# Eight cos/sin tables issued by ScalarE, the x pieces alone in SyncE's queue, and new instruction orders, in a spectral mixer with a gated FFN on one core

## The chip, the core and the metric

The kernel runs on one core of one Trainium2 chip. The metric is the device time of one execution in microseconds, as the median of several runs. A further execution is recorded by the hardware profiler; its own time stands beside its span below, since all durations come from it.

## The reference

The input x has 2048 rows of 576 numbers (bf16). Two blocks follow one another, each on a layer norm and with a residual:

```python
def _A_ref(x, w_r, w_i):
    X = rfft2(x.astype(float32), axes=(-2, -1))
    X = X * (w_r + 1j * w_i)
    return irfft2(X, s=(S, D), axes=(-2, -1)).astype(bfloat16)

def _B_ref(x, w_gate, w_up, w_down):
    return (gelu(x @ w_gate) * (x @ w_up)) @ w_down      # 576 -> 4608 -> 576

h  = x + _A_ref(layernorm(x), w_r, w_i)
h2 = h + _B_ref(layernorm(h), w_gate, w_up, w_down)
```

## The kernel before

The rows lie as 128 partitions by 16 tiles (tile c holds row 16p + c on partition p), in the buffer `XO`. Both Fourier transforms and their inverses are matrix products with tables of cosines and sines. The work has these stages, one behind the other with overlap:

- **First transform, groups 0 to 5** (`GROUPS`: tiles 0-1, 2-3, 4-6, 7-9, 10-12, 13-15). The layer norm is folded into the table: per tile, the mean and variance are found, the group's reciprocal of the standard deviation is taken, and the table `ATB` is multiplied by it into `ATS`. PE then multiplies x with `ATS` (line 537). Negated and tail copies of x go to `XN` for that.
- **Spectral stage**, 16 groups of frequencies: D (line 611) multiplies with `FT`, B (621) with `BT`, T, Z on VectorE apply the weights `WS` (w, line 635, makes their negated copy, in four parts `w0` to `w3`), V (651) and R (663) go back with `VT`.
- **Inverse and second norm** for the first six tiles: the matmuls of line 736 and 779, then transposes.
- **FFN** in four blocks of 512 rows: gate and up products (line 877), Gelu on ScalarE, product on VectorE, down product (line 978). The other ten tiles' inverse is done inside the first block.

Nothing is scheduled at run time. Each engine executes its instructions in the order in which the program records them, and a recording layer (`Prog`) turns reads and writes of named keys into semaphore waits. Three strings give the order. `LORD` lists the first loads: `x0-2` is the piece of x with tiles 0 and 1, `a0-4` the tables of tiles 0 to 3. `SEQ1` orders the first transform, `SEQF` the spectral stage. A word of `SEQ1` is a letter, a number and sometimes an engine (A ScalarE, D VectorE, P GpSimd):

| word | what it records | line |
|---|---|---|
| B, b | statistics of the first and second half of a tile, VectorE | 480 |
| S, Q | sum and sum of squares of a tile on ScalarE (tiles 3, 4, 13) | 472, 476 |
| m | the squared mean of such a tile | 483 |
| v, q, c | aggregate (VectorE), square root (ScalarE), reciprocal (VectorE) of a group | 489/492, 496, 501 |
| n, t | negated copy and tail copy of a group's x, GpSimd | 553, 558 |
| x | scaling of a group's tables, GpSimd (P) or VectorE (D) | 506, 511 |
| M | matmuls of a group | 537 |
| E, F | eviction of a finished bank (F: its second half, late) | 548 |
| k | idle matmuls on zeros: `k14` is 14 of them | 522 |

All loads before the FFN weights are issued by SyncE in one queue: the words of `LORD`, then `FT` and `BT`, the spectral weights in two halves, `VT`, `DT`, `IT`, `DP`, `ITD`, `IDT`. ScalarE issues no DMA. Its first instruction is a one-element square root (line 431), ahead of which the activation table is loaded. Two small constants, `EXQ` and `MK` (six memsets, lines 417 to 420), are set by VectorE; `EPT` and `ZD` by GpSimd.

Of the kernel before, what the change touches and what calls it, by code (L numbers as in the profile page):

```python
# [9 lines left out]
S, D, K2 = 2048, 576, 289  # L10
# [10 lines left out]
NPRE = 6  # L21
PARTS = ((0, 256), (256, 512))
GROUPS = ((0, 2), (2, 4), (4, 7), (7, 10), (10, 13), (13, 16))
SEQ1 = """S3 B0 t1 b0 b1 B1 v0 q0 c0 Q3 n0 m3D B2 k14 t0 x0P b2 n1 v1 q1 n2 k104 c1 B5 S4 m4P b5 Q4 B6 M0 E1A b6 v2 B7 x1P E0A M1 E4A q2 E5A t2 b7 c2 B9 E3A x2P E2A E8A E6A b8 S13 B8 b9 v3 q3 k202 M2 B11 B10 n3 n4 c3 x3P E12A b10 b12 E9A b11 B12 v4 E13A Q13 E7A q4 E10A t3 E11A B15 m13P E14A M3 t4 c4 E15A E16A b14 x4P M4 B14 b15 t5 v5 E17D q5 E18A E21A n5 E19A c5 x5D E20D E22D E23A E24A F23A F24A M5 E27A E25D E29A F29A E26D E28D F28A F25D F27D F22A F26D""".split()
LORD = "x0-2 x2-4 a0-4 x4-8 a4-8 x8-12 x12-16 a8-16".split()
SPLIT = tuple(int(w[1:-1]) for w in SEQ1 if w[0] == "F")
ACT_TILES = tuple(int(w[1:]) for w in SEQ1 if w[0] == "Q")
SEQF = """D0 D1 w0 D2 B0 T0 D3 B1 Z0 D4 T1 Z1 B2 V0 T2 B3 D5 T3 B4 D6 w1 Z2 T4 Z3 D7 B5 D8 w3 B6 w2 D9 T5 Z4 B7 Z5 T6 B8 R0 D11 T7 V2 Z7 D10 V1 B9 T8 B10 D13 Z6 V4 T9 T10 R1 D12 V3 Z8 B11 B12 Z9 D14 T11 V6 B13 T12 V5 B14 Z11 V7 Z10 T13 D15 Z12 T14 V8 Z13 V9 B15 Z14 R2 T15a V12 V10 T15b Z15a V11 Z15b V13 V14 R3 V15 R4""".split()
VENG = [('act',), ('act',), ('act',), ('act',), ('act',), ('act',), ('act',), ('act',), ('act',), ('act',), ('act',), ('act',), ('act',), ('act',), ('act',), ('act', 'act')]
DENG, BENG = ['act', 'act', 'act', 'act', 'act', 'act', 'act', 'act', 'act', 'act', 'act', 'act', 'act', 'act', 'act', 'act'], ['act', 'act', 'act', 'act', 'act', 'act', 'act', 'act', 'act', 'act', 'act', 'act', 'act', 'act', 'act', 'act']  # L30
SEQ = """I0 I1 N0 I2 s0 N1 I3 S1 q0 N2 I4 c0 e0 s2 q1 n0 n1 N3 I5 c1 z0 n2 s3 e1 D1 N4 N5 e2 q2 c2 n3 e3 D2 g10 g00 h10 z3 h00 g20 g01 h20 h01 g21 g11 h21 h11""".split()
# [281 lines left out]
def _build(nc, A_x, A_w_r, A_w_i, B_w_gate, B_w_up, B_w_down, out):  # L313
    P = Prog(nc)
    T = build_tables()
    dram = {n: nc.inline_tensor(_np_bf16(T[n]), name="c_" + n.lower()) for n in T}
    PE, DVE, ACT, SP, POOL = "pe", "dve", "act", "sp", "pool"
# [4 lines left out]
    XO = sb.alloc("XO", [128, NT, D], BF16)  # L322
# [35 lines left out]
    EXQ = sb.alloc("EXQ", [128, NT], F32)  # L358
    NM = sb.alloc("NM", [128, NT], F32)
    MK = sb.alloc("MK", [128, 4], F32)  # L360
# [24 lines left out]
    ATB = sb.alloc("ATB", [128, NT, 128], BF16)  # L385
# [28 lines left out]

    P.op(POOL, lambda g: g.memset(EPT[:, :], EPS), w=["EPT"])
    P.op(POOL, lambda g: g.memset(ZD[:, :], 0.0), w=["ZD"])
    P.op(DVE, lambda g: g.memset(EXQ[:, :], -0.5), w=["EXQ"])
    P.op(DVE, lambda g: g.memset(MK[:, :], 0.0), w=["MK"])
    for j in range(4):
        P.op(DVE, lambda g, j=j: g.memset(MK[32 * j:32 * j + 32, j:j + 1], 1.0), w=["MK"])  # L420
    xv = A_x[0].rearrange("(p c) d -> p c d", c=NT)
    ov = out[0].rearrange("(p c) d -> p c d", c=NT)
    tabs = dram["ATAB"].rearrange("p (c k) -> p c k", c=NT)

    def x_load(i, c0, c1, eng):
        P.dma(eng, XO[:, c0:c1, 0:D], xv[:, c0:c1, :], f"ld{i}", w=[("X", c) for c in range(c0, c1)])

    def atb_load(i, c0, c1, eng):
        P.dma(eng, ATB[:, c0:c1, :], tabs[:, c0:c1, :], f"ld{i}", w=[("ATB", c) for c in range(c0, c1)])

    P.op(ACT, lambda a: a.activation(SA[:, 0, 0:1], EPT[:, 0:1], ACTF.Sqrt), r=["EPT"], w=[("SA0", 0)])
    for i, w in enumerate(LORD):
        c0, c1 = (int(v) for v in w[1:].rstrip("@").split("-"))
        (x_load if w[0] == "x" else atb_load)(i, c0, c1, ACT if w[-1] == "@" else SP)
    P.dma(SP, FT[:, :, :].rearrange("p a b -> p (a b)"), dram["FTAB"][:, :], "ft", w=["FT"])
    P.dma(SP, BT[:, :, :, :].rearrange("p a b c -> p (a b c)"), dram["BTAB"][:, :], "bt", w=["BT"])

# [41 lines left out]
    def ln1_half(c, h):  # L479
        P.op(DVE, lambda v: v.bn_stats(ST1[:, c, h, :], XO[:, c, 288 * h:288 * h + 288]), r=[("X", c)], w=[("ST1", c, h)])  # L480
# [59 lines left out]
    def a_ev(n, eng, late=False):  # L540
        i, k = n // 5, AORD[n % 5]
        hs = (1,) if late else (0,) if n in SPLIT else (0, 1)
        g0, g1 = 8 * hs[0], 8 * hs[-1] + 8
        c0, c1 = GROUPS[i]
        m, b = c1 - c0, a_bank(i, k)
        src = bank(b, 0, 128, 0, 128 * m).rearrange("p (n g e) -> p n g e", n=m, g=16)[:, :, g0:g1, :]
        dst = U[:, k, g0:g1, c0:c1, :].rearrange("p g n e -> p n g e")
        fn = (lambda v: v.tensor_copy(dst, src)) if eng == DVE else (lambda a: a.activation(dst, src, ACTF.Copy))  # L548
        P.op(eng, fn, r=[("PS", b)] + ([("EV", n)] if late else []), w=[("U", i, k, h) for h in hs] + ([] if late else [("EV", n)]))
# [12 lines left out]
    RUN1 = {"k": idle_mm, "S": act_sum, "Q": act_sq, "B": lambda c: ln1_half(c, 0), "b": lambda c: ln1_half(c, 1), "v": ln1_var, "q": ln1_sqrt, "c": ln1_rs, "M": a_mm, "x": ln1_scale, "E": a_ev, "F": lambda n, eng: a_ev(n, eng, True), "n": x_neg, "m": act_mean2, "t": x_tail}  # L562
    for w in SEQ1:
        a = w[1:]
# [3 lines left out]
    c = 0  # L568
    while c < NT:
        c1 = c + 1  # L570
        while c not in ACT_TILES and c1 < NT and c1 not in ACT_TILES:
            c1 += 1
        src, f, keys = (SA[:, 0, c:c1], -1.0 / D, "SA0") if c in ACT_TILES else (MV1[:, c:c1, 0], -1.0, "MV1")
        P.op(POOL, lambda g, c=c, c1=c1, src=src, f=f: g.tensor_scalar(NM[:, c:c1], src, f, 1.0, op0=ALU.mult, op1=ALU.mult),
             r=[(keys, k) for k in range(c, c1)], w=[("NM", k) for k in range(c, c1)])
        c = c1
# [5 lines left out]
    FB, used = {}, [0] * 8  # L582
    for t, w in enumerate(SEQF):
        k, i = w[0], w[1:].rstrip("abc")
        if k in "DB":
            late = ("V", 0) in FB or any(x[0] == "V" for x in SEQF[t:t + 4])
            b = min((0, 2, 4) if late else (0, 2, 4, 6), key=lambda b: max(used[b], used[b + 1]))
            used[b] = used[b + 1] = t + 1
        elif k in "VR":
            b = min((6, 7) if ("D", LAST) not in FB else range(8), key=lambda b: used[b])  # L590
            used[b] = t + 1
            if k == "V":
                b2 = b
                if int(i) == LAST and len(VENG[LAST]) > 1:
                    b2 = min(range(8), key=lambda b: used[b])
# [79 lines left out]

    for w in SEQF:
        i = int(w[1:].rstrip("abc"))
# [43 lines left out]
    for t, w in enumerate(SEQ):  # L721
        k, i = w[0], int(w[1:])
# [294 lines left out]
def bass_sequential_preLN__spectral_gfnet__geglu_ffn__prompt_kernel(  # L1017
    nc, A_x, A_w_r, A_w_i, B_x, B_w_gate, B_w_up, B_w_down, out
):
    _build(nc, A_x, A_w_r, A_w_i, B_w_gate, B_w_up, B_w_down, out)  # L1020
# [28 lines left out]
```

## Time and profile before

| what | value |
|---|---|
| median of 3 runs | 490.87 us (490.7 to 491.16) |
| the profiled execution | 491.02 us |
| its span, first to last instruction | 489.2 us |
| PE busy | 481.8 us, 98% |
| VectorE, ScalarE, GpSimd busy | 193.6, 150.7, 32.1 us |
| granted PE clock, mean | 1.000 |
| read from HBM, written | 26.22 MB, 2.36 MB |

A line of a timeline gives the start in microseconds from the span's start, the duration, the engine, the line of the program, the operation, what is written and read, and in brackets how long the engine stood idle before it and what ended that. The durations shown overlap a little on ScalarE and VectorE: an eviction of 0.65 us (line 603) is followed by the next at 0.55 us. The chain of waits is followed back from the last instruction, at each step to what released it.

### The profile page before, as it was taken

The page shows a single profiled execution, that of the slowest core. Times are in us where ns is not written, and L with a number is a line of the kernel's source. Part 1 is how long each engine was busy: PE and PEld are TensorE (multiplying, and loading weights), DVE is VectorE, ACT ScalarE, POOL GpSimd, SP SyncE. Part 2 cuts the span into 40 slices and gives each one's busy share as a digit, 9 for nine tenths or more (in the row PEclk, how much of TensorE's full clock was granted, in tenths as well). Part 3 has the DMA queues.
Part 4 walks back from the last instruction along what each step waited for, and adds up shares of the span by engine and source line. Part 5 has one row for each costly group of instructions (what it writes and reads, how often), then busy time and mean ns, then how long its engine had stood idle before and what let it go on. Part 6 is the DMA issues. An engine that isn't in the chain of part 4 may idle for free.

```text
span 489.2 us, 9939 instructions
## 1 busy us (share of the span) xinstructions
PE 481.8 (98%) x4376; PEld 286.3 (59%) x4376; DVE 193.6 (40%) x399; ACT 150.7 (31%) x297; POOL 32.1 (7%) x60
## 2 busy tenths in 40 slices
PE   7899999999999999999999999999999999999998
PEld 3787754444688744444577644444677544444775
DVE  6799733433576634433311144333211233333111
ACT  6999742233322223323200032233100122323000
POOL 5511441000000020000000000000000000000000
PEclk9999999999999999999999999999999999999999
DMA  8990999100001071100000001000000000000000
GB/s 283 231 325 16 365 366 340 26 15 2 1 19 40 13 233 23 24 4 1 2 18 19 13 20 22 16 0 1 7 19 19 7 1 0 1 2 1 13 20 18
DMA packets 25148, 31.20 MB, mean 64 GB/s; under 512 B 11440, under 2 KB 17840, under 8 KB 25104
## 3 DMA queue, kind: packets, MB, share of 16 engines
q1 hardware_dynamic: 22208, 18.62, 13.4%
q0 software_dynamic: 2896, 11.95, 7.0%
q8 instruction: 34, 0.56, 0.5%
q14 instruction: 10, 0.08, 0.1%
HBM read 26.22 MB, written 2.36 MB: 58 GB/s over the span
## 4 chain that ended last, share of the span: by engine, by line
PE 92%; ACT 3%; DVE 3%; DMA 1%; issue 0%; SPq 0%; POOL 0%; DVEq 0%
PE PS L877 57%; PE PS L978 29%; PE PS L537 1%; DMA XO<-in_A_x_dram 1%; DVE TP L630 1%; PE PS L895 1%; ACT V L603 1%; PE PS L736 1%; ACT YS L603 1%; PE PS L611 1%; PE PS L779 1%; PE PS L913 1%; ACT U L548 0%; DVE VR L666 0%; ACT CUS L603 0%
## 5 line engine op out<-in xcount | busy, mean ns | idle before, releaser
L877 PE MATMUL PS<-HT,WG 64*128 64x512 bf16 (+1 forms) x2160 | 228.7, 371 | 0.0
L877 PEld LDWEIGHTS PS<-HT,WG 64*128 64x128 bf16 x2160 | 105.0, 94 | 121.9 <-issue 0.7
L886 DVE TENSOR_TENSOR AT<-GL,PS 128x512 bf16<-128x512 bf16 (+1 forms) x147 | 99.4, 677 | 177.9 <-ACT GL L885 177.9
L885 ACT ACTIVATE GL<-PS 128x512 bf16<-128x512 f32 (+1 forms) x147 | 86.5, 588 | 262.6 <-PE PS L877 251.3
L978 PE MATMUL PS<-WD,AT 128*128 128x288 bf16 (+2 forms) x1152 | 144.9, 286 | 0.0
L978 PEld LDWEIGHTS PS<-WD,AT 128*128 128x128 bf16 x1152 | 110.7, 98 | 30.6 <-ACT GL L885 0.8
L877 PE MATMUL PS<-HT,WGX 64*128 64x512 bf16 x486 | 53.4, 376 | 0.0
L981 DVE TENSOR_TENSOR OS<-PS,XO 128x288 bf16<-128x288 f32 (+2 forms) x32 | 14.6, 457 | 94.4 <-PE PS L978 94.3
L877 PEld LDWEIGHTS PS<-HT,WGX 64*128 64x128 bf16 x486 | 23.7, 94 | 28.8
L611 PE MATMUL PS<-FT,U 128*128 128x288 bf16 x96 | 13.9, 286 | 0.0
L630 DVE TENSOR_TENSOR TP<-YS,WS 128x1152 bf16<-128x1152 bf16 (+2 forms) x17 | 12.0, 719 | 2.7 <-ACT YS L603 2.5
L900 ACT ACTIVATE EB<-PS 128x288 f32<-128x288 f32 x10 | 4.1, 411 | 27.6 <-PE PS L895 27.6
L537 PE MATMUL PS<-ATS,XO 128*128 128x128 bf16 x96 | 8.6, 219 | 3.1 <-POOL ATS L506 1.6
L480 DVE BATCH_NORM_STATS2 ST<-XO 128x6 f32<-128x288 bf16 x26 | 10.0, 441 | 2.7 <-DMA XO<-in_A_x_dram 2.7
L918 DVE TENSOR_TENSOR XO<-PS,XO 128x576 bf16<-128x576 f32 x10 | 7.6, 756 | 8.0 <-PE PS L913 8.0
L611 PEld LDWEIGHTS PS<-FT,U 128*128 128x128 bf16 x96 | 9.2, 98 | 2.3
L603 ACT ACTIVATE CUS<-PS 128x576 bf16<-128x576 f32 x16 | 10.4, 659 | 0.5 <-PE PS L611 0.3
L603 ACT ACTIVATE YS<-PS 128x576 bf16<-128x576 f32 x16 | 10.3, 664 | 0.4 <-DVE TP L630 0.4
L621 PE MATMUL PS<-CUS,BT 128*128 128x288 bf16 x64 | 10.0, 286 | 0.0
L548 ACT ACTIVATE U<-PS 128x256 bf16<-128x256 f32 (+2 forms) x29 | 9.6, 417 | 0.7 <-PE PS L537 0.6
L906 DVE TENSOR_TENSOR QB<-PS,EB 128x288 f32<-128x288 f32 x20 | 8.2, 452 | 3.3 <-ACT EB L900 3.3
L823 DVE TENSOR_SCALAR HN<-XO,NM,RS 128x576 bf16<-128x576 bf16 (+1 forms) x28 | 9.2, 369 | 0.1
(80 smaller groups left out, 207.6 us busy)
## 6 DMA issues: line engine op xcount, KB each, us to landing
WD<-in_B_w_down_dram POOLq DMA_DIRECT2D x9, 576.0 KB, 12.0
WG<-in_B_w_up_dram SPq DMA_DIRECT2D x4, 1152.0 KB, 7.8
WG<-in_B_w_gate_dram POOLq DMA_DIRECT2D x4, 1152.0 KB, 10.2
out_dram<-OS SPq DMA_DIRECT2D x30, 72.0 KB, 1.6
XO<-in_A_x_dram SPq DMA_DIRECT2D x3, 576.0 KB, 7.4
WGX<-in_B_w_up_dram SPq DMA_DIRECT2D x1, 1152.0 KB, 6.0
WGX<-in_B_w_gate_dram POOLq DMA_DIRECT2D x1, 1152.0 KB, 10.0
HT<-HN SPq DMA_TRANSPOSE x60, 2.4
```

The lines of the kernel that those rows point to most:

```text
L480: P.op(DVE, lambda v: v.bn_stats(ST1[:, c, h, :], XO[:, c, 288 * h:288 * h + 288]), r=[("X", c)], w=[("ST1", c, h)])
L537: P.op(PE, lambda t, b=b, lhs=lhs, s=s, e=e, o=o, c=c: t.matmul(bank(b, 0, 128, o, o + 128), lhs, ATS[:, c, :], start=s, stop=e), r=[("X", ...
L548: fn = (lambda v: v.tensor_copy(dst, src)) if eng == DVE else (lambda a: a.activation(dst, src, ACTF.Copy))
L603: fn = (lambda v: v.tensor_copy(dst, src)) if eng == DVE else (lambda a: a.activation(dst, src, ACTF.Copy))
L611: P.op(PE, lambda t, b=b, m=m, us=us, o=o: t.matmul(bank(b, 0, 128, 0, 2 * HK), U[:, us, i, :, :], FT[:, 3 * o + (2 if us == 4 else us // ...
L621: P.op(PE, lambda t, b=b, tb=tb, m=m, s3=s3, sp_=sp_: t.matmul(bank(b, 0, 128, 0, KW), BT[:, sp_, tb, :], CUS[:, s3, m, :], start=(m == 0) ...
L630: P.op(DVE, lambda v: v.tensor_tensor(TP[:, tl, :, :, q0:q1], y4, w4, op=ALU.mult), r=[("Y", sl), ("Wn", i)] + (wkeys[0] if 1 <= g < 9 els ...
L877: op = P.op(PE, lambda t, h0=h0, kt=kt, wt=wt, b=b, s=(not second and j == 0), e=(second and j == n - 1): t.matmul(bank(b, 0, 128, c0, c1) ...
L885: P.op(ACT, lambda a: a.activation(GL[:, s2, c0:c1], bank(b0, 0, 128, c0, c1), ACTF.Gelu_apprx_tanh), r=[("PS", b0)], w=[("GL", s2)])
L886: P.op(DVE, lambda v: v.tensor_tensor(AT[:, f, c0:c1], GL[:, s2, c0:c1], bank(b0 + 1, 0, 128, c0, c1), op=ALU.mult), r=[("GL", s2), ("PS", ...
L978: P.op(PE, lambda t, b=b, d0=d0, d1=d1, f=f, p=p: t.matmul(bank(b, 0, 128, 0, d1 - d0), AT[:, f, 128 * p:128 * p + 128], WD[:, f, d0:d1], ...
L981: P.op(DVE, lambda v, b=b, d0=d0, d1=d1, p=p, c=c: v.tensor_tensor(OS[:, p % 2, d0:d1], bank(b, 0, 128, 0, d1 - d0), XO[:, c, d0:d1], op=A ...
```

## The change

1. `LORD` is new. SyncE's queue now has x0-2, x2-4, x4-8, x8-12, the tables 8-16, x12-16. The tables 0-4 and 4-8 are issued by ScalarE; a new read key makes them wait for the one-element square root.
2. The six memsets of `EXQ` and `MK` go from VectorE to GpSimd.
3. `SEQ1` and `SEQF` have new orders. The number of instructions of each kind stays the same; the squared mean of tile 3 goes from VectorE to GpSimd (`m3D` to `m3P`), and the evictions are dealt out anew between ScalarE and VectorE.

```diff
-SEQ1 = """S3 B0 t1 b0 b1 B1 v0 q0 c0 Q3 n0 m3D B2 k14 t0 x0P b2 n1 v1 q1 n2 k104 c1 B5 S4 m4P b5 Q4 B6 M0 E1A b6 v2 B7 x1P E0A M1 E4A q2 E5A t2 b7 c2 B9 E3A x2P E2A E8A E6A b8 S13 B8 b9 v3 q3 k202 M2 B11 B10 n3 n4 c3 x3P E12A b10 b12 E9A b11 B12 v4 E13A Q13 E7A q4 E10A t3 E11A B15 m13P E14A M3 t4 c4 E15A E16A b14 x4P M4 B14 b15 t5 v5 E17D q5 E18A E21A n5 E19A c5 x5D E20D E22D E23A E24A F23A F24A M5 E27A E25D E29A F29A E26D E28D F28A F25D F27D F22A F26D""".split()
-LORD = "x0-2 x2-4 a0-4 x4-8 a4-8 x8-12 x12-16 a8-16".split()
+SEQ1 = """S3 n0 b0 B0 b1 t1 B1 v0 q0 b2 c0 Q3 n1 B2 m3P v1 q1 B6 k104 t0 x0P t2 c1 x1P b5 B7 k14 S4 B5 m4P Q4 b6 B8 M0 E4A E1A E0A v2 M1 E7A E3A B9 q2 b7 E9A c2 E2A n2 E8A E6A b8 S13 B11 b9 v3 q3 b10 k202 E5A n3 B12 x2P c3 M2 E10A E11A t4 Q13 t3 B10 b11 b12 v4 q4 m13P E13A x3P b15 c4 b14 E14A B14 B15 n4 x4P v5 E12A M3 E16A E15A E17D q5 E18A c5 n5 x5D M4 E20D E19A E22A E23A F23A E21D t5 M5 E25A E27D E24A F24D E29D E26A F25A F26D F27D E28A F29D F22D F28A""".split()
+LORD = "x0-2 x2-4 x4-8 x8-12 a8-16 x12-16 a0-4@ a4-8@".split()
...
-SEQF = """D0 D1 w0 D2 B0 T0 D3 B1 Z0 D4 T1 Z1 B2 V0 T2 B3 D5 T3 B4 D6 w1 Z2 T4 Z3 D7 B5 D8 w3 B6 w2 D9 T5 Z4 B7 Z5 T6 B8 R0 D11 T7 V2 Z7 D10 V1 B9 T8 B10 D13 Z6 V4 T9 T10 R1 D12 V3 Z8 B11 B12 Z9 D14 T11 V6 B13 T12 V5 B14 Z11 V7 Z10 T13 D15 Z12 T14 V8 Z13 V9 B15 Z14 R2 T15a V12 V10 T15b Z15a V11 Z15b V13 V14 R3 V15 R4""".split()
+SEQF = """D1 w1 w0 D0 D2 B1 B0 T1 T0 Z0 D3 D4 Z1 B2 D5 w3 T2 w2 B3 T3 Z3 B4 T4 D6 B5 D8 D7 B6 V0 Z4 V1 Z2 T5 B7 T6 B8 Z6 R0 D9 V2 D10 V3 T7 B9 Z5 T8 Z7 B10 D11 T9 V4 Z9 T10 D12 R1 B11 Z8 T11 V6 D13 Z11 B12 T12 D14 B13 V5 Z10 T13 B14 V7 T14 Z12 D15 V8 Z13 V9 Z14 B15 R2 V10 T15a V13 V11 T15b Z15a Z15b V14 V12 R3 V15 R4""".split()
...
-    P.op(DVE, lambda g: g.memset(EXQ[:, :], -0.5), w=["EXQ"])
-    P.op(DVE, lambda g: g.memset(MK[:, :], 0.0), w=["MK"])
+    P.op(POOL, lambda g: g.memset(EXQ[:, :], -0.5), w=["EXQ"])
+    P.op(POOL, lambda g: g.memset(MK[:, :], 0.0), w=["MK"])
     for j in range(4):
-        P.op(DVE, lambda g, j=j: g.memset(MK[32 * j:32 * j + 32, j:j + 1], 1.0), w=["MK"])
+        P.op(POOL, lambda g, j=j: g.memset(MK[32 * j:32 * j + 32, j:j + 1], 1.0), w=["MK"])
...
-        c0, c1 = (int(v) for v in w[1:].rstrip("@").split("-"))
-        (x_load if w[0] == "x" else atb_load)(i, c0, c1, ACT if w[-1] == "@" else SP)
+        c0, c1 = (int(v) for v in w[1:].rstrip("@!").split("-"))
+        (x_load if w[0] == "x" else atb_load)(i, c0, c1, ACT if w[-1] in "@!" else SP, {"@": [("SA0", 0)], "!": [("X", 0)]}.get(w[-1], []))
```

More of the change, by code (lines that the diff above doesn't have):

```diff
@@ L423, in _build, with x_load, atb_load @@
     tabs = dram["ATAB"].rearrange("p (c k) -> p c k", c=NT)
[L425 to L429, printed above, removed]
+    def x_load(i, c0, c1, eng, r):
+        P.dma(eng, XO[:, c0:c1, 0:D], xv[:, c0:c1, :], f"ld{i}", r=r, w=[("X", c) for c in range(c0, c1)])
+    def atb_load(i, c0, c1, eng, r):
+        P.dma(eng, ATB[:, c0:c1, :], tabs[:, c0:c1, :], f"ld{i}", r=r, w=[("ATB", c) for c in range(c0, c1)])
     P.op(ACT, lambda a: a.activation(SA[:, 0, 0:1], EPT[:, 0:1], ACTF.Sqrt), r=["EPT"], w=[("SA0", 0)])
     for i, w in enumerate(LORD):
-        c0, c1 = (int(v) for v in w[1:].rstrip("@").split("-"))
-        (x_load if w[0] == "x" else atb_load)(i, c0, c1, ACT if w[-1] == "@" else SP)
+        c0, c1 = (int(v) for v in w[1:].rstrip("@!").split("-"))
+        (x_load if w[0] == "x" else atb_load)(i, c0, c1, ACT if w[-1] in "@!" else SP, {"@": [("SA0", 0)], "!": [("X", 0)]}.get(w[-1], []))
     P.dma(SP, FT[:, :, :].rearrange("p a b -> p (a b)"), dram["FTAB"][:, :], "ft", w=["FT"])
```

## The prediction

> **What bounds the kernel now.** I read the page first, then the chain of waits in order of time, then POOL's timeline, then the DMA rate by stretches.
>
> ```profile
> span 489.2 us, 9939 instructions
> PE 92%; ACT 3%; DVE 3%; DMA 1%; issue 0%; SPq 0%; POOL 0%; DVEq 0%
> ```
>
> PE carries the chain, and a change that removes no matmul can gain only where the chain leaves PE. The chain in order of time shows where that is.
>
> ```profile
> 2.11 5.87 DMA XO<-in_A_x_dram
> 7.98 0.02 issue
> 8.01 1.55 DVE ST L480 x4
> 9.56 0.62 POOL ATS L506
> ...
> 15.27 4.83 PE PS L537 x81
> 20.10 2.21 PE PS L611 x18
> ...
> 48.34 1.63 PE PS L736 x12
> ```
>
> Columns: start, length, what. The first link is the third x piece (tiles 4 to 7), issued at 2.11 and landed at 7.98. From 48.34 on PE runs almost without a break to the end at 489.2, in an order that the change leaves alone. So the change is worth what it does to the start of the first L736 matmul, 48.34. That stretch has two parts: up to the first L611 matmul (19.93 in the timeline), and 28.4 us after it.
>
> The chain view hides who paces the first part. POOL's timeline shows it (start, length, line, tile, idle before):
>
> ```profile
> 8.06 0.91 POOL L553 TENSOR_SCALAR XN<-XO 128x864 bf16<-128x864 bf16 x1 [0.54 <-DMA XO<-in_A_x_dram]
> 9.14 0.26 POOL L483 TENSOR_SCALAR TM<-SA 128x1 f32<-128x1 f32 x1 [0.18 <-POOL XN L553]
> 9.56 0.61 POOL L506 TENSOR_TENSOR ATS<-ATB,RS 128x256 bf16<-128x256 bf16 x1
> 10.26 0.27 POOL L558 TENSOR_SCALAR XN<-XO 128x96 bf16<-128x96 bf16 x1
> 10.82 0.83 POOL L506 TENSOR_TENSOR ATS<-ATB,RS 128x384 bf16<-128x384 bf16 x1 [0.29 <-DVE RS L501]
> 11.81 0.91 POOL L553 TENSOR_SCALAR XN<-XO 128x864 bf16<-128x864 bf16 x1 [0.16 <-POOL ATS L506]
> ...
> 13.96 0.83 POOL L506 TENSOR_TENSOR ATS<-ATB,RS 128x384 bf16<-128x384 bf16 x1 [0.17 <-POOL XN L553]
> 14.88 0.27 POOL L558 TENSOR_SCALAR XN<-XO 128x96 bf16<-128x96 bf16 x1
> ...
> 16.02 0.83 POOL L506 TENSOR_TENSOR ATS<-ATB,RS 128x384 bf16<-128x384 bf16 x1
> ```
>
> From the landing at 7.98 to the scaling of group 4 (x4P, 16.02) POOL only pauses 0.08 (one wait) or about 0.16 (several) between instructions, and once 0.29. PE starts that group at 16.91 and goes on to 19.93: 3.91 us behind x4P's start. Hence x4P's start sets the first part, and the landing of x tiles 4 to 7 sets x4P.
>
> Why that piece lands at 7.98 shows in the DMA rates (last number, GB/s; the one before, DMA share):
>
> ```profile
> 2.50:4.25 1.75, 1.75 (x5) 0.61 (x4) 0.56 (x2) 0.00 (x0) 0.00 (x0) 1.00 1.21 380
> 4.25:5.25 1.00, 1.00 (x3) 0.30 (x2) 1.00 (x4) 0.78 (x2) 0.57 (x2) 1.00 0.56 104
> 5.25:8.00 2.75, 2.75 (x20) 1.50 (x19) 1.68 (x9) 1.25 (x4) 1.88 (x4) 1.00 0.95 339
> 8.00:12.50 4.50, 2.65 (x40) 2.08 (x38) 4.49 (x18) 4.28 (x14) 3.58 (x6) 1.00 1.02 400
> ```
>
> There is a hole from 4.25 to 5.25. Issue start plus time to landing, asked issue by issue, gives: x0-2 3.67, x2-4 4.44, tables 0-4 4.74, x4-8 7.98, tables 4-8 8.76, x8-12 10.46, x12-16 11.91, tables 8-16 12.57. The hole begins where the queue goes from the first tables to x4-8.
>
> **The change part by part.**
>
> *SyncE's queue.* Two issues of 0.47 us go from ahead of x8-12, one of them from ahead of x4-8, so x4-8 is issued 0.47 and x8-12 0.95 earlier. That alone brings nothing: the engines were moving earlier pieces. What counts is the bytes ahead and the hole. Ahead of x4-8, after x2-4, there stood 131 kB of tables; now up to 262 kB come through the other queue beside it. Early end: no hole, 262 + 590 kB at 400 GB/s from 4.44 = 6.6. Late end: the hole stays and 131 kB more pass, 7.98 + 0.33 = 8.3. The nearest row is x12-16, an x piece directly behind an x piece as x4-8 now is: 1.45 us. With 0.3 for each table (as tables 0-4 took) that is 4.44 + 2.05 = 6.5. I take at most 7.0. FT, BT and the weights move about 0.9 us up; they landed from 14.6 to 26.5, before their first use, and are worth nothing. Without that cover the next is the negation w3, which moves from 29.65 to about 25 and needs the weights that landed at 24.40: 0.6 us of cover.
>
> *ScalarE's queue.* Two issues behind the 0.20 us Sqrt that ends at 2.22. No row shows a DMA issued by ACT; SP's rows are 0.43, POOL's up to 0.98. ACT then is free at 3.1 to 4.2, and its next instruction waits for x at 4.46: nothing, with 0.3 us of cover at the worst end. Tables 0-4 are issued 0.6 later than before (2.25 for 1.64). POOL needs them at 6.4, before they landed 3.1 after issue: 5.4. One microsecond of cover.
>
> *Memsets.* Six tiny ones move from DVE to POOL, 0.06 to 0.1 each and 0.08 apart, ending near 2.5. POOL first works on x at 3.75. Nothing; 1.2 us of cover.
>
> *POOL's order.* It now runs n0, t1, n1, m3P, t0, x0P, t2, x1P, m4P, n2, n3, x2P, t4, t3, m13P, x3P, n4, x4P. m3P is new on POOL (0.26 and a pause of 0.16); t4 comes ahead of x4P as before. x1P has two predecessors:
> - On POOL: n0 ends at 4.42, t1 starts at 4.6 (x2-4 at 4.44; 4.8 if the tables push it to 4.74). t1 0.24, n1 0.67, m3P 0.26, t0 0.24, x0P 0.61, t2 0.27 are 2.29; six pauses of 0.08 or 0.16 are 0.8. x1P at 7.7 to 7.9.
> - Over DVE: the reciprocal for x1P now stands behind B6, a statistic of x4-8. Landing L, 0.02 to start, 0.36 spacing, 0.17 reciprocal, 0.12 to POOL: L + 0.67. At L = 7.0, 7.7.
>
> From x1P on nothing waits for another engine if x8-12 lands by 9.8 and x12-16 by 11.9: 0.61 + 0.26 + 0.91 + 0.91 + 0.83 + 0.27 + 0.27 + 0.26 + 0.83 + 0.91 = 6.06, and ten pauses, 1.39: 7.45. So x4P at 15.15 to 15.35; I take 15.25, against 16.02: **0.77 us gained**. Next late is POOL itself: earlier data brings no more. Group 5's scaling on DVE (17.73 before) has to end by 17.7 for PE; by the same rows it just does.
>
> *The second part.* D, B, T, Z, V, R get a new order with the same instructions. ACT has 32 evictions at a spacing of 0.55 and 16 at 0.48, 25.3 of the 28.4 us. I laid both orders out, each instruction at the later of its engine's spacing and its inputs: 28.2 us each way, the new one 0.04 shorter (the trace's 28.4 has 0.2 of wait at the first L736 matmul, which stays). Bounds: 0.5 either way, a quarter of the idle time that the layout leaves on ACT (1.9). I take 0.
>
> **Sum.** The profiled execution took 491.02, 489.2 of it span; less 0.77 it is 490.25. It lies 0.15 above the median 490.87, so the median goes to **490.1**. A change under 0.2% (0.98 us) is about what a measurement of this kernel can't tell from none, so this forecast counts as "the same", by a small margin.
>
> **Rivals.**
>
> *The hole is not the tables' doing.* Then L = 8.3: x1P at 8.97, x4P at 16.42, 0.4 us later than before: 491.3. Break-even is L = 7.9. For it: nothing in the trace says what made the hole, and as many bytes stand ahead of x8-12 as before. If only x8-12 keeps its 10.46, n3 starts at 10.54 and x4P 5.27 behind it (its share of the sum above) at 15.81, a gain of 0.2. Against: the later join of an x piece to an x piece shows no hole. The Trainium skill, "DMA: Bandwidth & Descriptors", section "Issuing engines are not separate DMA queues", speaks against the change here: DMAs of different issuing engines run interleaved on the same 16 DMA engines, and a second issuer saves issuing time only. By that rule the bytes ahead of x8-12 decide, which is the case of 10.46 above; this trace has a single hardware queue in these microseconds and can't show it.
>
> *The tables land late.* In their own queue they could take turns packet by packet with the x pieces and land with x4-8. x0P then waits for tables 0-4, and x4P starts 8.7 us behind that landing plus 0.08. Break-even is a landing at 7.25; at 8.3 it costs 1.05: 491.9, slower by over 0.2%. For it: eight packets a DMA engine against eight. Against: x2-4 is still moving at 3.3, when table packets can start (x0-2's began 1.0 after issue), so they share with that first.
>
> *More is gained.* The second part closes up by the 0.5 bound too: 489.6. For it: ACT's idle time. Against: the layout shows no such thing.
>
> **How the numbers follow.** Forecast 0.60, hole stays 0.18, late tables 0.12, more gained 0.10. One execution's jitter (the three runs lie 0.46 apart, and a DVE scaling took 0.53 for 0.24 once) puts a fifth of the forecast, 0.12, beyond 0.98, and all of "more": faster 0.22. Slower: 0.10 of the late tables and 0.05 of the hole case (with x8-12 late too): 0.15. The same: 0.63. The range goes from 489.6 ("more") to 491.5 (hole case and 0.2 of jitter), leaving out the late tables and the tails.
>
> **What would show it.** Right: x4-8 landing before 7.2, POOL without idle time beyond 0.2 from 4.6 to x4P, x4P near 15.25, the first L611 matmul near 19.15, the first L736 near 47.55, and 28.4 between them. Wrong: x1P behind a DVE release after 8 (hole), x0P behind a DMA of the tables (late tables), an ACT start after 4.5 behind its issues, or more than 28.7 in the second part.

## The result and the profile after

The change makes the kernel slower: 493.47 us (492.94 to 494.19, six runs) against 490.75 us (490.5 to 491.16, six runs) for the kernel before. The ratio is 1.0056, with a 95% interval of 1.0043 to 1.0069: 2.1 to 3.4 us lost. The profiled execution took 493.26 us.

The page of the changed kernel, its span, its second hardware queue and its chain:

```profile
span 491.5 us, 9938 instructions
q10 hardware_dynamic: 288, 0.26, 0.2%
PE 95%; DMA 1%; POOL 1%; ACT 1%; issue 0%; DVE 0%; POOLq 0%
```

The span grew by 2.3 us. q10 is new: 0.26 MB, the tables that ScalarE issues. The chain in order of time (start, length, what) no longer begins with a piece of x:

```profile
2.25 7.22 DMA ATB<-c_atab
9.55 0.62 POOL ATS L506
10.74 0.62 POOL ATS L506
...
19.19 3.17 PE PS L537 x54
22.36 2.22 PE PS L611 x18
...
50.58 1.63 PE PS L736 x12
```

It begins with tables 0-4: issued at 2.25, landed at 9.47. The first L736 matmul starts at 50.58 instead of 48.34. That is 2.24 us, the whole difference between the two profiled executions (493.26 less 491.02). The medians lie 2.7 us apart; two of the six executions of the changed kernel had a mean granted clock of 0.997 and are the longest, at 494.1 and 494.2 us. POOL's timeline shows who paid:

```profile
6.09 0.24 POOL L558 TENSOR_SCALAR XN<-XO 128x64 bf16<-128x64 bf16 x1
9.55 0.61 POOL L506 TENSOR_TENSOR ATS<-ATB,RS 128x256 bf16<-128x256 bf16 x1 [3.21 <-DMA ATB<-c_atab]
10.32 0.27 POOL L558 TENSOR_SCALAR XN<-XO 128x96 bf16<-128x96 bf16 x1 [0.16 <-POOL ATS L506]
...
18.21 0.83 POOL L506 TENSOR_TENSOR ATS<-ATB,RS 128x384 bf16<-128x384 bf16 x1
```

x0P could have started at 6.4. It waited 3.21 us for the tables, and everything behind it on POOL waited with it, although x2-4 was there at 4.40 and x4-8 at 8.45. x4P starts at 18.21, 8.66 behind x0P, and 2.19 later than before. From the first L611 matmul (22.20 in PE's timeline) to the first L736 matmul it is 28.4 us, as before.

The DMA rate by the same stretches as before (last number GB/s, the one ahead of it the DMA share):

```profile
2.50:4.25 1.75, 1.75 (x5) 0.61 (x4) 0.56 (x2) 0.00 (x0) 0.50 (x1) 1.00 1.00 392
4.25:5.25 1.00, 1.00 (x4) 0.39 (x3) 1.00 (x4) 0.78 (x2) 0.76 (x3) 1.00 1.01 387
5.25:8.00 2.75, 2.02 (x10) 0.70 (x8) 1.39 (x7) 1.26 (x4) 0.83 (x3) 1.00 0.95 320
```

The hole from 4.25 to 5.25 is gone: 387 GB/s where it was 104. So the transfers did become faster there, and the kernel slower. The bytes that came sooner were not the ones that POOL waited for. x4-8 as a whole even landed later than before, at 8.45 for 7.98, and x8-12 at 10.25 for 10.46.

### The profile page after: what moved, and what is told of

It reads as the page before. It is cut to its first block, busy times and chain, and to the rows that moved or that the text cites. A ratio compares the mean times of both kernels' runs of the same rounds, so it can differ in the third digit from the quotient of the medians.

```text
span 491.5 us, 9938 instructions
## 1 busy us (share of the span) xinstructions
PE 481.7 (98%) x4375; PEld 286.2 (58%) x4376; DVE 193.9 (39%) x393; ACT 151.2 (31%) x296; POOL 32.8 (7%) x67
## 4 chain that ended last, share of the span: by engine, by line
PE 95%; DMA 1%; POOL 1%; ACT 1%; issue 0%; DVE 0%; POOLq 0%
PE PS L877 57%; PE PS L978 29%; PE PS L611 2%; PE PS L621 2%; DMA ATB<-c_atab 1%; PE PS L651 1%; PE PS L895 1%; PE PS L736 1%; PE PS L537 1%; PE PS L779 1%; ACT U L548 1%; PE PS L913 0%; POOL ATS L506 0%; POOL XN L553 0%; PE PS L841 0%
## 5 line engine op out<-in xcount | busy, mean ns | idle before, releaser
L611 PE MATMUL PS<-FT,U 128*128 128x288 bf16 x96 | 13.7, 286 | 0.0
L611 PEld LDWEIGHTS PS<-FT,U 128*128 128x128 bf16 x96 | 9.3, 98 | 2.3
L537 PEld LDWEIGHTS PS<-ATS,XO 128*128 128x128 bf16 x96 | 6.8, 98 | 6.3 <-POOL ATS L506 5.3
```

The lines of the kernel that those rows point to most:

```text
L537: P.op(PE, lambda t, b=b, lhs=lhs, s=s, e=e, o=o, c=c: t.matmul(bank(b, 0, 128, o, o + 128), lhs, ATS[:, c, :], start=s, stop=e), r=[("X", ...
L611: P.op(PE, lambda t, b=b, m=m, us=us, o=o: t.matmul(bank(b, 0, 128, 0, 2 * HK), U[:, us, i, :, :], FT[:, 3 * o + (2 if us == 4 else us // ...
```

## The experiments

In the short names, "old loads" is the old `LORD`, "new orders" the new `SEQ1` and `SEQF` with the moved memsets. Ratios are against the kernel before on the same chip, whose median there was 490.68 to 491.01 us. In the kernels with packed tables and in run 6 the program's lines shift by one (L506 becomes L507). All times are us from the span's start.

| kernel | median | ratio (95%) | tables 0-4 | x4-8 | x0P | x4P | first L736 |
|---|---|---|---|---|---|---|---|
| before | 490.75 | | 4.74 | 7.98 | 6.14 | 16.02 | 48.34 |
| changed | 493.47 | 1.0056 (1.0043 to 1.0069) | 9.47 | 8.45 | 9.55 | 18.21 | 50.58 |
| 1 old loads, new orders | 491.21 | 1.0005 (0.9996 to 1.0014) | 5.95 | 7.90 | 6.57 | 16.01 | 48.55 |
| 2 new loads, old orders | 496.05 | 1.0105 (1.0088 to 1.0122) | 9.38 | 7.54 | 9.45 | 19.84 | 52.35 |
| 3 tables issued at 0.72 | 491.73 | 1.0015 (1.0005 to 1.0024) | 4.63 | 7.43 | 8.04 | 16.73 | 49.17 |
| 4 tables 0-8 in one piece | 491.73 | 1.0015 (1.0005 to 1.0024) | 6.26 | 7.89 | 6.44 | 15.99 | 48.38 |
| 5 as 1, tables packed | 490.65 | 0.9994 (0.9985 to 1.0004) | 5.48 | 7.34 | 6.60 | 15.47 | 48.03 |
| 6 as 1, tables touched early | 491.35 | 1.0013 (1.0004 to 1.0022) | 5.45 | 7.70 | 6.57 | 15.84 | 48.22 |
| 7 as 3, tables packed | 491.24 | 1.0007 (0.9998 to 1.0017) | 3.88 | 6.98 | 7.29 | 15.99 | 48.38 |
| 8 x4-8 issued with the tables | 493.11 | 1.0047 (1.0031 to 1.0064) | 9.02 | 8.84 | 9.09 | 17.78 | 50.19 |
| 9 changed, tables packed | 493.49 | 1.0048 (1.0034 to 1.0062) | 9.64 | 8.18 | 9.72 | 18.98 | 51.35 |
| 10 before, tables packed | 490.77 | 0.9991 (0.9982 to 1.0000) | 5.19 | 7.78 | 6.22 | 15.80 | 48.12 |
| 11 changed, once more | 493.79 | one run | 9.86 | 7.82 | 9.93 | 18.72 | 51.10 |
| 12 as 5, once more | 490.64 | 0.9990 (0.9981 to 0.9999) | 5.17 | 7.05 | 6.48 | 15.21 | 48.12 |

The table is ordered as the runs were made. It is read here by question. Small differences in it need care: some executions had a mean granted clock of 0.993 to 0.997 and not 1.000. Of the kernel before it was 16 of the 71 beside runs 1 to 12, and they took about 1 us longer than the others.

### Which part of the change costs it

The change is cut in two. Run 1 keeps the new orders and takes the loads back:

```diff
-LORD = "x0-2 x2-4 x4-8 x8-12 a8-16 x12-16 a0-4@ a4-8@".split()
+LORD = "x0-2 x2-4 a0-4 x4-8 a4-8 x8-12 x12-16 a8-16".split()
```

> The changed kernel with the old LORD: all tables and x pieces in SyncE's queue as before; new orders and the memsets on GpSimd stay. Theory 1 (the loss is the late landing of tables 0-4 from ScalarE's queue, nothing else): tables 0-4 land near 4.7 again, x4-8 near 8.0, the scaling of group 4 (x4P) starts at 16.4 and the first L736 matmul near 48.7; 0.3 to 0.4 us slower than before. Rival 1 (the new orders or the memsets cost the time): 2.0 to 2.7 us slower than before, as the change.

Run 2 keeps the new loads and has the old `SEQ1` and `SEQF`:

```diff
-SEQ1 = """S3 n0 b0 B0 b1 t1 ... F28A"""
+SEQ1 = """S3 B0 t1 b0 b1 B1 ... F26D"""
-SEQF = """D1 w1 w0 D0 ... R4"""
+SEQF = """D0 D1 w0 D2 ... R4"""
```

> The changed kernel with the old SEQ1 and SEQF: only the loads and the memsets are new. Theory 1: tables 0-4 land near 9.5, the first scaling on GpSimd (x0P) starts right behind them, and the whole loss is there: 2 to 3 us slower than before. Rival 1 (the orders): within 0.3 us of before.

Run 1 takes the time of the kernel before within its interval, -0.2 to +0.7 us. The new orders and the memsets cost nothing that can be measured, and the loads cost all of it. (The expectation had x4P 0.4 us too late.) Run 1 also shows what the hole does. The rate from 4.25 to 5.25 is 96 GB/s there, and POOL, in the new order, waits for x4-8 as it did before:

```profile
7.98 0.27 POOL L558 TENSOR_SCALAR XN<-XO 128x96 bf16<-128x96 bf16 x1 [0.80 <-DMA XO<-in_A_x_dram]
8.53 0.61 POOL L506 TENSOR_TENSOR ATS<-ATB,RS 128x256 bf16<-128x256 bf16 x1 [0.28 <-DVE RS L501]
...
16.01 0.83 POOL L506 TENSOR_TENSOR ATS<-ATB,RS 128x384 bf16<-128x384 bf16 x1
```

x4P starts at 16.01 with x4-8 at 7.90, beside 16.02 with 7.98 in the kernel before: with the old loads the two orders of POOL are worth the same.

Run 2 is 5.1 us slower than before, where 2 to 3 were expected. The late tables hit the old order harder:

```profile
9.45 0.61 POOL L506 TENSOR_TENSOR ATS<-ATB,RS 128x256 bf16<-128x256 bf16 x1 [3.62 <-DMA ATB<-c_atab]
...
19.84 0.83 POOL L506 TENSOR_TENSOR ATS<-ATB,RS 128x384 bf16<-128x384 bf16 x1 [1.16 <-DVE RS L501]
```

The old order has n1, n2 and m4 between x0P and x1P, so that x1P starts at 12.48, where it is 10.74 in the changed kernel. In the end POOL even waits for a reciprocal of VectorE. So the new orders are what makes the new loads bearable, not what makes them slow.

### Why the tables land late

Three causes stood against each other: ScalarE's queue is served behind SyncE's; it was issued too late; the tables' own layout makes it slow.

Run 3 issues both tables from ScalarE ahead of the square root and its activation table, at 0.72 and 1.12:

```diff
-    P.op(ACT, lambda a: a.activation(SA[:, 0, 0:1], EPT[:, 0:1], ACTF.Sqrt), r=["EPT"], w=[("SA0", 0)])
...
-        (x_load if w[0] == "x" else atb_load)(i, c0, c1, ACT if w[-1] in "@!" else SP, {"@": [("SA0", 0)], "!": [("X", 0)]}.get(w[-1], []))
+        (x_load if w[0] == "x" else atb_load)(i, c0, c1, ACT if w[-1] in "@!" else SP, [])
+    P.op(ACT, lambda a: a.activation(SA[:, 0, 0:1], EPT[:, 0:1], ACTF.Sqrt), r=["EPT"], w=[("SA0", 0)])
```

> The changed kernel with ScalarE's two table issues ahead of the square root and its table load, without a wait: issued near 0.7 instead of 2.25. Theory 2 (the tables are late because the x pieces were already queued on every DMA engine when they came): first table packets before 2.5, tables 0-4 landed by 4.2, x0P no later than 6.6; then the landing of x4-8 decides: between 0.6 us faster (landing up to 7.2) and 0.6 us slower (8.5) than before. Rival 2 (ScalarE's queue is served behind SyncE's, however early it is issued): tables 0-4 land after 6.5, at least 0.3 us slower than before, as the change if they land at 9.5.

The tables land at 4.63 (4.2 was expected), so ScalarE's queue is not served behind SyncE's as such. But the x pieces pay: x0-2 lands at 4.92 and x2-4 at 6.03, for 3.66 and 4.40 in the changed kernel. POOL's row names it:

```profile
6.10 0.24 POOL L558 TENSOR_SCALAR XN<-XO 128x64 bf16<-128x64 bf16 x1 [0.42 <-DMA XO<-in_A_x_dram]
```

x0P comes at 8.04, where 6.6 at the latest was expected, and x4P at 16.73. The kernel is 0.15% slower than before (0.05 to 0.24%).

Run 8 leaves the tables where the change has them and holds x4-8 back, so that SyncE issues it at 2.25 too, and what stands behind it 0.5 us later than the changed kernel does:

```diff
-        (...)(i, c0, c1, ACT if w[-1] in "@!" else SP, {"@": [("SA0", 0)], "!": [("X", 0)]}.get(w[-1], []))
+        (...)(i, c0, c1, ACT if w[-1] in "@!" else SP, [("SA0", 0)] if w[-1] == "@" or w == "x4-8" else [])
```

> The changed kernel, where SyncE's issue of x4-8 also waits for ScalarE's square root, so that x4-8 is issued at 2.25 with the tables and not at 1.64 ahead of them. Theory 2 (the DMA engines had x4-8 and x8-12 queued before the tables came): table packets start by 4.8, tables 0-4 land by 6.5, x0P by 6.6, and the time is between 0.8 us faster and 0.4 us slower than before. Rival 2' (0.6 us of issue make no difference; tables start only when an engine is through with x4-8): tables 0-4 land after 8, at least 1 us slower than before.

The tables landed at 9.02 and the kernel is 2.3 us slower than before: the figures are those of the rival, not of the theory (6.5). The rival's reason does not hold, for the first table row began at 3.87, and the first engine was through with x4-8 at 5.93. Which packets move when says more. The queues' packets in the changed kernel (packets, MB, share of 16 engines), in the stretch from 2.25 to 5.75:

```profile
q1 hardware_dynamic: 440, 1.27, 97.2%
```

And in the stretch from 5.75 to 9.5:

```profile
q1 hardware_dynamic: 332, 1.09, 74.4%
q10 hardware_dynamic: 272, 0.25, 24.0%
```

Not one packet of the tables moved in the 3.5 us after they were issued. Their first began at 5.75, when most DMA engines had finished x4-8: a load gives one signal from each of the 16 engines, and for x4-8 fourteen of these came between 5.42 and 5.82. In run 8, with x4-8 issued at the same time as the tables, the stretch from 3.75 to 6.25 has both:

```profile
q1 hardware_dynamic: 95, 0.36, 65.3%
q10 hardware_dynamic: 67, 0.06, 10.1%
```

So x4-8 issued 0.6 us ahead was through on most engines before the first table row, and issued together with the tables it did not (nor did x0-2 in run 3). Why 0.6 us is enough for that, no run shows. In run 8 the two queues then take turns, about row by row: each signal of tables 0-4 comes about 0.2 us behind one of x4-8 (5.93 and 6.12 the first, 8.84 and 9.02 the last). A row of x takes 0.18 us (4608 bytes), a row of the tables 0.05 (1024 bytes), eight of each lie on an engine; with such turns the small load ends where the large one does.

In the changed kernel the tables stood behind x4-8, and at first behind x8-12 too, which was issued 0.14 us ahead of them: from 5.75 to 6.25 SyncE's queue moved 38 packets and ScalarE's 7, from 6.25 to 7.5 each moved 92. The first engine was through with x8-12 at 6.97 and with tables 0-4 at 7.71; the fourteenth signal of the tables came at 8.72, the last at 9.47. The 131 kB that POOL needs first thus waited for the 590 kB of x4-8 and then went beside and behind the 590 kB of x8-12. Without the head start of x4-8 (run 8) they landed only 0.45 us sooner: taking turns with a large load makes them late enough.

Run 9 asks for the third cause. The tables lie in DRAM as one array with 4096 bytes from row to row; it has them as three arrays without gaps:

```diff
-    T["ATAB"] = A.reshape(128, 16 * 128)
+    A = A.reshape(128, 16 * 128)
+    T["AT0"], T["AT4"], T["AT8"] = A[:, :512], A[:, 512:1024], A[:, 1024:]
...
-        P.dma(eng, ATB[:, c0:c1, :], tabs[:, c0:c1, :], f"ld{i}", r=r, w=[("ATB", c) for c in range(c0, c1)])
+        P.dma(eng, ATB[:, c0:c1, :], tabs[c0][:, :, :], f"ld{i}", r=r, w=[("ATB", c) for c in range(c0, c1)])
```

> The changed kernel, with its tables in DRAM as three separate tensors without gaps between rows (tiles 0-3, 4-7, 8-15), everything else as it is. Theory (the second queue is the cause: its packets come behind and then one for one with those of the x pieces, so the tables land with x4-8 or later, wherever they lie in DRAM): tables 0-4 land at 8.5 or later, x4P 8.74 behind that, at 17.2 or later, at least +1.2 us on the kernel before; 492 or more. Rival (the gaps between the rows are the cause, as they were for part of the hole in the old loads): tables 0-4 land by 7, x4P by 15.8, 490.7 or less.

The tables landed at 9.64 all the same, and the time is that of the changed kernel. Run 11 is the changed kernel a second time:

> The changed kernel once more, for a second profile. Theory (queues that take turns): first packets of the tables about 5.5 to 6, tables 0-4 landed at 8.5 to 9.5, x4P 8.7 behind. Rival (the late landing was one slow DMA engine in that one execution): tables 0-4 landed before 8, x4P before 16.8.

Its first table packet began at 5.23, its tables landed at 9.86. The lateness is no accident of one execution. So neither a lower rank of ScalarE's queue nor the tables' layout makes them late, but the large loads that are issued ahead of them or with them.

### What the hole is

The prediction left open whether the tables made the hole. Run 4 puts the tables 0 to 7 into one piece, with rows of 2048 bytes, in SyncE's queue:

```diff
+LORD = "x0-2 x2-4 a0-8 x4-8 x8-12 a8-16 x12-16".split()
```

> The new orders, all loads in SyncE's queue: x0-2 x2-4 a0-8 x4-8 x8-12 a8-16 x12-16, so tables 0-8 are one piece with rows of 2048 bytes in place of two with 1024. Theory 3 (the hole at 4.25 to 5.25 in the kernel before comes from the rows of 1024 bytes ahead of x4-8): no stretch of 1 us under 300 GB/s between 3 and 8, tables by 5.2, x4-8 by 7.4: 0.3 to 0.7 us faster than before. Rival 3 (any change from table rows to x rows makes it): the hole is there, x4-8 after 8.0, 0.2 to 0.6 us slower than before.

The hole stays (145 GB/s from 4.25 to 5.25), x4-8 lands at 7.89: the hole does not need rows of 1024 bytes. (Its median is 0.7 us above that of its profiled execution, 491.07, which was its shortest; the table's landings are of that one.)

Run 6 reads 16 bytes of every table row from ScalarE at 0.72, ahead of the tables' own load:

```diff
+    P.dma(ACT, JNK[:, 0, 0:8], tabs[:, 0, 0:8], "tch", w=["J0"])
```

> New orders and the loads as in the kernel before, and ScalarE issues one tiny load (16 bytes of each table row) ahead of its square root, at 0.7. Rival 4 (first touch): the hole moves to the first 3 us, where little moves yet; x0-2 and x2-4 land up to 0.7 later, and x4-8 lands by 7.2: between 0.7 faster and 0.3 slower than before. Theory 4 (rows 4096 apart): the hole stays between 4.2 and 5.5, x4-8 near 7.9, 0.2 to 0.4 us slower than before.

The hole stays (78 GB/s): it is not the first touch of the tables' rows. Run 5 packs them as in run 9, in the old loads:

> New orders, all loads in SyncE's queue as in the kernel before, but the tables lie in DRAM as three packed tensors, one for each load, so a load's 128 rows follow one another instead of standing 4096 bytes apart. Theory 4 (the hole behind the first tables comes from rows of one table load all standing 4096 bytes apart): no stretch under 300 GB/s between 3 and 8, tables 0-4 by 4.8, x4-8 by 7.0, x4P near 15.2: 0.6 to 0.8 us faster than before. Rival 4 (the hole comes from the first touch of the tables' memory, wherever its rows lie): the hole stays, x4-8 near 7.9, within 0.4 us of before.

Here the hole shrinks, less than expected (x4-8 lands at 7.34 and not at 7.0). The window row of run 5 for that stretch:

```profile
4.25:5.25 1.00, 1.00 (x3) 0.30 (x2) 1.00 (x4) 0.77 (x2) 0.76 (x3) 1.00 0.76 211
```

And that of run 1, whose tables are not packed:

```profile
4.25:5.25 1.00, 1.00 (x3) 0.30 (x2) 1.00 (x4) 0.78 (x2) 0.76 (x3) 1.00 0.48 96
```

Runs 10 and 12 had 274 and 275 GB/s. With the old loads x4-8 lands at 7.05 to 7.78 packed, and at 7.70 to 7.98 (runs 1, 6 and the kernel before) unpacked. The distance between the tables' rows is thus part of the hole. The time goes into single rows of x: in the kernel before, the ten rows of x4-8 that began between 4.0 and 4.5 took 1.0 us each on the mean, where 0.18 is usual. Run 7 has run 3's early tables packed:

> The tables issued first by ScalarE as in the run e3, now from the packed tensors. Theory 4: the low stretch from 2.5 to 4.25 (221 GB/s in e3) is gone, x2-4 lands by 5.2 instead of 6.0, x4-8 by 6.8: 0.2 to 0.5 us faster than before. Rival 4: as e3, 0.8 us slower than before.

With the tables first in time the hole lies earlier, from 2.0 to 3.4 (115 GB/s in run 3, 243 in run 7). It follows the tables: in the changed kernel, too, the rate falls to 272 GB/s from 6.5 to 7.5, when their rows move. Packing makes it smaller; what makes the rest of it stays open. The gain that was expected of run 7 did not come (ratio 1.0007).

### The tables packed, with the old orders and with the new

Runs 10 and 12 were made side by side: the kernel before packed, and run 5 again.

> The kernel before, with its tables in DRAM as three separate tensors without gaps between rows, everything else as it is. Theory (the gaps cost part of the hole behind the first tables, and the landing of x4-8 sets POOL, as the prediction read it): x4-8 lands at 7.3 to 7.5 in place of 7.98, x4P at 15.4 to 15.6 in place of 16.02, 0.4 to 0.6 us faster than the kernel before: 490.2 to 490.5. Rival (only the new order uses the earlier data, since the old one waits elsewhere on POOL): x4P stays within 0.2 of 16.02, the time within 0.3 of the kernel before.

> The old loads with the tables packed and the new orders, once more and with its tables in the same state, now beside the kernel before packed alone. Theory (packing is worth 0.4 to 0.6, the new orders about nothing): within 0.3 us of the kernel before packed alone, 490.2 to 490.7. Rival (the orders cost 0.5, as the run with the new orders alone left open with 0.2 +- 0.45): 0.4 or more above it.

They take 490.77 and 490.64 us, ratios 0.9991 and 0.9990. Run 10 lies between its two expectations: x4-8 at 7.78, later than forecast, and x4P 0.22 earlier than before. The two are within 0.13 us of each other, so the new orders are worth nothing beside the packing, either. The lowest medians are those of runs 5 and 12: old loads, packed tables, new orders. By their ratios they gain 0.3 and 0.5 us on the kernel before, with intervals that end at 1.0004 and 0.9999. Most of that is the clock: none of their 21 executions had a mean granted clock below 1.000, and of the kernel before 3 of 25 and 7 of 21 had. Whether the kernel has a part in that is not shown. The medians of the executions at 1.000 alone are 490.66 for 490.67 (run 5) and 490.64 for 490.83 us (run 12). So a gain on the kernel before is not shown. On the changed kernel it is about 2.5 us (493.12 less 490.64, both at 1.000).

## Why the prediction was wrong

**The step that failed** is a term that had been given cover and no price: "before they landed 3.1 after issue: 5.4. One microsecond of cover." It carried the landing time of a load that stood third in one queue over to a load that stood in another queue, 0.6 us behind 590 kB. They landed 7.2 us after issue. The two halves of the mistake: the first packet was expected at about 3.3, one microsecond after issue, "so they share with that first", and came at 5.75; then going beside and behind the rows of x8-12 took till 7.7 on the quickest engine and 9.47 on the slowest. The prediction's own sign for this case came, x0P behind a DMA of the tables.

**The rival that named it had the right sum.** "x4P starts 8.7 us behind that landing plus 0.08": 9.47 and 8.78 are 18.25, measured 18.21. Its break-even, 7.25, follows from the same sum. Its size, a landing with x4-8 at 8.3, and its chance, 0.12, were too small. It reasoned with one x piece of company. The tables first stood behind one, and then shared with the next; and in run 8, with one for company, they landed at 9.02.

**What held.** The hole did go away, and was the tables' doing, at least in the sense that it follows them. The hole-free rate held, and fourteen of sixteen engines had x4-8 at 5.82, even ahead of the forecast 6.5 to 7.0; that was luck, for the forecast had tables moving beside it, and none did. The sum from x0P to x4P on POOL held within 0.04 us; the sum from x1P (10.74) gives 7.47 for 7.45. ScalarE was free at 3.07 and started on x at 4.42, memsets ended at 2.33: nothing lost, as stated. The second part took 28.4 us, as stated.

**A second step failed, hidden behind the first.** The prediction took x4-8 at 7.0 at most. A piece lands with its last engine, and that one took till 8.45 (7.54 to 8.45 in the four executions with these loads: the changed kernel and runs 2, 9 and 11). VectorE's statistic B6 and the reciprocal for x1P stood behind it:

```profile
8.47 0.46 DVE L480 BATCH_NORM_STATS2 ST<-XO 128x6 f32<-128x288 bf16 x1 [1.76 <-DMA XO<-in_A_x_dram]
8.85 0.15 DVE L501 RECIPROCAL RS<-RS 128x2 f32<-128x2 f32 x1
```

By the prediction's own sums, L + 0.67 for x1P and 7.45 more for x4P, a landing at 8.45 gives 9.12 and 16.57: 0.55 us later than before, even with the tables in time. When x4-8 would land with the tables in time, no run with these loads shows.

**The gain itself was too large.** Run 12 reached the forecast's x4P (15.21 for 15.25) by another way, 0.81 us ahead of the kernel before, but its first L736 matmul came at 48.12, only 0.22 earlier, and its profiled execution was 0.20 us shorter (490.82 for 491.02). The prediction said "Next late is POOL itself". The chain of run 12 shows another:

```profile
16.16 9.58 DMA WS<-in_A_w_i_dram
...
25.77 0.40 DVE WS L636
```

A piece of the spectral weights landed at 25.74, and VectorE's negation of it waited for that. The prediction had named this wait as the next one if the weights were not issued earlier, with 0.6 us of cover on a landing at 24.40. In run 12 the weights are issued as late as before, and that piece came 1.3 us later than 24.40. Whether the changed kernel's earlier issue (15.85 for 16.16) would have covered it is not shown: its weights landed at 24.92, but by then everything else was 2 us later. VectorE stood idle for 0.44 us at this wait, and the second part took 28.9 us in run 12's profile where it was 28.4 before: of the 0.73 us won at the first L611 matmul (19.20 for 19.93), 0.22 were left.

## What to carry to other kernels

Before a load is moved to another engine's queue, ask who is issued ahead of it in time, in every queue: in these runs, position in a queue protected a small, urgent load from the large ones behind it, and a second queue took that protection away. Price it as the bytes issued ahead plus a turn-by-turn share with the bytes that follow, and take the slowest DMA engine, not the mean rate. And when a gap in the transfer rate is the target, ask which bytes fill it: a full rate is worth nothing if the consumer waits for others.

## What the runs showed of the hardware

**A second queue waits first, then alternates.** In the four executions with the changed loads no packet of the second queue moved for 2.8 to 3.6 us, behind a piece issued 0.6 us earlier (3.5 us in the changed kernel). Issued together with that piece (run 8), rows of 1024 and 4608 bytes went about in turn. The Trainium skill, "DMA: Bandwidth & Descriptors", section "Issuing engines are not separate DMA queues", says that the queues of different issuers run interleaved on the same engines; the rows of 5.75 to 9.5 (74.4% and 24.0%) agree, the first 3.5 us don't.

**The spread between DMA engines is part of a load's time.** In the changed kernel x4-8's signals came from 5.42 to 8.45; in run 12, with the old loads, from 5.95 to 7.05.

**PE's clock fell behind some of its waits.** In the second execution of the changed kernel (run 11) and in run 9 the granted clock fell to half when PE, after its idle matmuls, had waited for the first scaled tables. The window rows from 11 to 13 of run 11 (granted clock third from the end):

```profile
11.00:12.00 1.00, 1.00 (x14) 1.00 (x12) 0.00 (x0) 0.00 (x0) 0.70 (x2) 0.57 1.09 411
12.00:13.00 1.00, 1.00 (x13) 1.00 (x10) 0.72 (x3) 0.73 (x3) 0.92 (x2) 0.50 1.05 211
```

PE had stood still for 3.7 us before that, and for 2.2 us in run 9; in the profiled execution of the changed kernel it stood still for 3.0 us and kept its clock at 1.00. The length of the pause alone does not decide it. The Trainium skill, "TensorE: Matmul & The Clock Gate", section "Part 1: The HAM clock gate", tells of a free-running window of about 3.4 us, after which an idle array goes to half its clock; the 2.2 us of run 9 do not fit an idle window of that length. In run 9 the first eviction came late behind the slow matmuls, POOL waited 0.76 us for a reciprocal that stood behind it, and x4P came 9.26 us after x0P instead of 8.66: there the fall cost 0.6 us more. Run 2 shows the same fall of the clock from 13 on, which may be part of its excess; all four of its executions had a mean clock of 0.993 to 0.997. That the late tables cause the fall is not shown: the kernel before had such executions too, and run 8, whose tables land at 9.02, had none among four.
